# Two products of an attention kernel on smaller tiles of the tensor engine: softmax times v in two column tiles, p' times w_in in eight tiles of 64 rows and 32 columns

## The chip, the cores and the metric

The kernel runs on one core of a Trainium2 chip. The time is device microseconds from start to end. Three runs of the kernel before gave 1541.19 to 1542.47, with a median of 1541.99. All data is fp32. In the profile PE is the tensor engine (PEld its weight loads), DVE the vector engine, ACT the scalar engine, POOL the GpSimd engine, SP the engine that issues most DMAs.

## The reference

Attention through 32 packed queries, then two feed-forward layers. The attention has 8 batches, 8 heads, 576 positions, 64 dimensions a head:

```python
def sm_attn(qq, kk, vv):
    s = scale * np.matmul(qq, kk.transpose(0, 1, 3, 2))
    s = s - np.max(s, axis=-1, keepdims=True)
    a = np.exp(s)
    a = a / (np.sum(a, axis=-1, keepdims=True) + 1e-09)
    return np.matmul(a, vv)
p_packed = sm_attn(p, k, v)            # p' : 32 x 64 for each head
out = sm_attn(q, p_packed, p_packed)   # 576 x 64 for each head
```

The output, as x of 4608 x 512, goes through `h = x @ w_in` (512 x 2048), a rational function of h, `@ w_out`, and then a second layer of the same sizes with a PReLU.

## The kernel before, in words

The second softmax's rows have 32 elements, one for each packed query. The kernel doesn't multiply them by p' and then by w_in; it multiplies p' of each head by that head's 64 rows of w_in once (the products W), and the first MoE layer then multiplies the softmax by this result. So h comes from a matrix of 256 rows (8 heads x 32) for each batch.

The attention runs in units. There are 16 half batches i of four heads, that is two pairs of heads (j = 0, 1 within the unit), and the loop over k (0 to 17) emits in every unit k work of several half batches, in the order of the letters in `ORDER`. For PE, DVE and ACT this comes to:

- s1 of half batch k (L308): scores of the packed queries, four products of 64 columns; DVE takes the maximum (`nm`), ACT the exp.
- T of k-1 (L320): five PE transposes of the exp, copied by ACT and DVE to `a1T`.
- P of k-2 (L333): exp times v. `pp` holds 128 rows (two pairs of heads of 2 x 32 queries) by 256 columns (four heads of 64), of which only the blocks of a head with itself are of use. DVE multiplies by the reciprocal of the sum and by a mask of zeros and ones (`ppn`, two operations of 64 rows). The result has, for a pair of heads, zeros where a head would meet the other's columns.
- R of k-2 (L347): PE transposes `ppn`, DVE copies it to `pph`.
- s2 of k-3 (L357): q times p'; DVE transposes in blocks of 32 (`trn`), takes the maximum, POOL subtracts it.
- E of k-4: ACT's exp, DVE's sums and reciprocal. A and B of k-5: DVE's product and transposes, SP's store to `a2_d`.
- W, four slots in each unit, here called slots 1 to 4: slot 1 stands behind s1, slot 2 behind E, slot 3 behind P, slot 4 behind s2.
- w: one step of the splitting of w_in or w_out (ACT and DVE, some POOL). In units 10 to 14 these are w_out's.
- K, V, Q: SP's loads of k, v and q.

The W products come in groups of 16 for a pair of batches. Units 6 to 9 emit those of the first pair (`emit_Wb0`, L395), units 10 to 13 those of the second, units 14 to 17 those of the third. The fourth pair's (`LAST`) are emitted in the drain (the list `DRAIN`) and in the first two steps of the MoE (`FILL`). From the second pair on, one product (L421) is a 128 x 128 block of p' (two batches, a pair of heads, half of it zeros) by 128 x 512 of w_in into one PSUM bank; ACT (in the last pair ACT and DVE by turns) copies it to `wbs`, and two such halves of 512 columns are stored together. The PSUM pool `psw` has two banks, so a slot's product waits until the bank of two slots before has been copied out.

Every engine works its instructions in the order in which they are emitted; waits are on semaphores. SP, too, issues its DMAs in order, and an issue that waits for data holds back those behind it.

The first MoE's loop starts with `load_a2(0)`, `split_a2(0)` and then L572; from there on nothing of the change is left but the last six W slots.

Of the kernel before, what the change touches and what calls it, by code (L numbers as in the profile page):

```python
# [11 lines left out]
F32 = mybir.dt.float32  # L12
# [4 lines left out]
AF = mybir.ActivationFunctionType  # L17
ALU = mybir.AluOpType
# [10 lines left out]
def attention_then_two_moes(ctx, tc, qT, kT, v, pT, w_in, w_out, ab, w2_in, w2_out, alpha, out):  # L29
    nc = tc.nc  # L30
    mm = nc.tensor.matmul
    act = nc.scalar.activation
    dve = nc.vector
    pool = nc.gpsimd
# [11 lines left out]
    LAST = B // 2 - 1  # L46
# [5 lines left out]
    wp = ctx.enter_context(tc.tile_pool(name="wp", bufs=8))  # L52
# [43 lines left out]
    opened = {}  # L96

    def open_pool(name, **kw):
        opened[name] = ExitStack()
        return opened[name].enter_context(tc.tile_pool(name=name, reuse_waits="tile", **kw))  # L100
# [4 lines left out]
    gp = open_pool("gp", bufs=1, side="left")  # L105
# [93 lines left out]
    spw = open_pool("spw", bufs=2, side="right")  # L199
    psw = open_pool("psw", bufs=2, space=PSUM, side="right")  # L200
    sp0 = open_pool("sp0", bufs=2, side="left")
    ps0 = open_pool("ps0", bufs=1, space=PSUM, side="left")

    ident = sp0.tile([128, 128], F32, tag="ident", name="ident", bufs=1)
    make_identity(nc, ident)
    mask = sp0.tile([128, 128], F32, tag="mask", name="mask", bufs=1)
    pool.memset(mask, 0.0)
    for h in range(4):
        o = 64 * (h % 2)
        pool.memset(mask[32 * h:32 * h + 32, o:o + 64], 1.0)  # L210

    pt, kt, qt, vt = {}, {}, {}, {}

# [21 lines left out]
    w_in_t = {}  # L235

    BLOCKS = [(j, c) for cp in (0, 2) for j in range(4) for c in (cp, cp + 1)]
    EARLY = NF // 2
    w_jobs = [(w_in[128 * j:128 * j + 128, 512 * c:512 * c + 512], plain, w_in_slot, True) for j, c in BLOCKS]
    w_done = []  # L240
# [52 lines left out]
    ps1, a1, rs1, a1T, ppn, ppt, pps, pph, tr, sm, a2 = ({} for _ in range(11))  # L293
# [4 lines left out]
    D = 3  # L298
# [34 lines left out]
    def emit_PP(i):  # L333
        pb = ps0.tile([128, 512], F32, tag="pp", name="pp")
        pps[i] = pb
        pp = pb[:, 0:256]
        at, v_ = a1T.pop(i), vt.pop(i)
        for c in range(5):
            kc = 128 if c < 4 else 64
            mm(pp, at[0:kc, c, :], v_[0:kc, c, :], start=c == 0, stop=c == 4)  # L340
        ppn[i] = sp0.tile([128, 128], F32, tag="ppn", name="ppn", bufs=1)
        for j in range(2):
            r = slice(64 * j, 64 * j + 64)
            dve.scalar_tensor_tensor(ppn[i][r, :], in0=pp[r, 128 * j:128 * j + 128],
                                     scalar=rs1[i][r, :], in1=mask[r, :], op0=ALU.mult, op1=ALU.mult)

    def emit_PPT(i):  # L347
        b, t = divmod(i, 2)
# [39 lines left out]
        b, t = divmod(i, 2)  # L388
        nc.sync.dma_start(out=a2_d[b][:, t, :], in_=a2.pop(i))

    wbs, stores = {}, []

    def emit_Wb0(n):


        f, bi = divmod(n, 2)
        pw = psw.tile([128, 2, 256], F32, tag="wb", name="pw")
        o = 256 * (f % 2)
        for jj, kt in COL:
            mm(pw[64 * jj:64 * jj + 64, kt, :], pph[0][:, 2 * kt + jj, bi, :],  # L400
               w_in_t[2 * kt + jj, f // 2][:, o:o + 256], start=True, stop=True)
        whole_t[bi, f] = wb_slot(NP * bi + f)
        t = whole_t[bi, f].rearrange("p h (k f) -> p h k f", k=2)
        act(t[:, 0], pw, AF.Copy)
        dve.tensor_tensor(t[:, 1], pw, t[:, 0], op=ALU.subtract)
        wb_t[bi, f] = t[:, 0], t[:, 1]

    def emit_Wb(n):
        bp, r = divmod(n, 16)
        if bp == 0:  # L410
            return emit_Wb0(n)
        j, fc = BLOCKS[r]
        if bp == LAST and r % 4 > 1 and "ps0" in opened:
            if fc % 2 == 0:
                wbs[1] = ps0.tile([128, 2, 512], F32, tag="s1", name="pw")
            pw = wbs[1][:, fc % 2, :]
        elif bp == LAST and r % 4 > 1:
            pw = psw2.tile([128, 512], F32, tag="wb", name="pw")
        else:
            pw = psw.tile([128, 512], F32, tag="wb", name="pw")  # L420
        mm(pw, pph[bp][:, j].rearrange("p a b -> p (a b)"), w_in_t[j, fc], start=True, stop=True)  # L421
        if fc % 2 == 0:
            if bp == LAST and r > 0:
                wbs[0] = wp.tile([128, 1024], F32, tag="D", name="wbs")
            elif bp == LAST or len(w_done) == len(w_jobs) and n % 4 == 0:
                wbs[0] = gp.tile([128, 1024], F32, tag="s4", name="wbs", bufs=3)
            else:
                wbs[0] = spw.tile([128, 1024], F32, tag="wbs", name="wbs")
        o = 512 * (fc % 2)
        if bp == LAST and n % 2:  # L430
            dve.tensor_copy(wbs[0][:, o:o + 512], pw)
        else:
            act(wbs[0][:, o:o + 512], pw, AF.Copy)  # L433
        if fc % 2:
            stores.append((bp, j, fc, wbs[0]))

    def store_Wb():
        while stores:
# [8 lines left out]
    def wb_step(k):  # L447
        store_Wb()
        n = nwb[0]
        if n < 16 * LAST and len(w_done) >= (16 if n >= 16 else 8 * (n // 8) + 8) and 4 * (n // 16) + 6 <= k:  # L450
            emit_Wb(n)
            nwb[0] += 1

    def each(f, i):
# [8 lines left out]
    stages = {  # L463
        "V": lambda k: each(load_v, k - 1), "Q": lambda k: each(load_q, k - D + 1), "K": lambda k: each(load_k, k + 2),
        "1": lambda k: each(emit_s1, k), "T": lambda k: each(emit_T, k - 1), "P": lambda k: each(emit_PP, k - 2),
        "R": lambda k: each(emit_PPT, k - 2), "2": lambda k: each(emit_s2, k - D), "E": lambda k: each(emit_exp2, k - D - 1),
        "A": lambda k: each(emit_a2, k - D - 2), "B": lambda k: each(store_a2, k - D - 2), "W": wb_step,
# [15 lines left out]
    for c in range(NCH):  # L483
        o, now = 0, []
        for i, n in enumerate(SHARES[c % 3]):
            b = VISITS[c + i]
# [49 lines left out]
    for c in DRAIN.split():  # L536
        if c == "W":
            store_Wb()
            emit_Wb(nwb[0])
            nwb[0] += 1  # L540
        elif c == "L":
            load_a2(0)
        elif c == "l":
            split_a2(0)
        elif c == "o":
            load_late(len(late_st))
        else:
            {"A": emit_a2, "B": store_a2, "S": emit_s2, "E": emit_exp2, "Q": load_q}[c[0]](NQ - int(c[1]))
# [9 lines left out]
    psw2 = open_pool("psw2", bufs=2, space=PSUM, side="right")  # L558
# [274 lines left out]
    for g in range(NG + LAG):  # L833
# [4 lines left out]
        if g < NG:  # L838
            c, f = divmod(g, NP)
            if f == 1 and c + 1 < NCH:  # L840
                load_a2(c + 1)
            emit_L1(g)
            for _ in range(FILL[g] if g < len(FILL) else 0):
                emit_Wb(nwb[0])
                nwb[0] += 1
# [185 lines left out]
    for u in range(len(units) + 2):  # L1031
        if u < len(units):
            s, y, i, n = units[u]
# [18 lines left out]
            if y == 0:  # L1052
                for g in range(2):
                    q = 0
                    for x, z in PASSES:
                        for k in range(2):
                            mm(ps[:, g, 0:m], w[:, g, x, 128 * k:128 * k + 128], ysp[s, i](z, k),  # L1057
                               start=not onto and q == 0, stop=q == 5, skip_group_check=again)
                            q += 1
            else:  # L1060
                t = vsp.pop(u)
                for g in range(2):
                    for d in range(2):
# [64 lines left out]
```

## Time and profile before

| | |
|---|---|
| median of three runs | 1541.99 us |
| profiled execution | 1541.61 us, span 1539.8 us |
| PE busy | 1472.9 us (96%) |
| DVE busy | 1307.6 us (85%) |
| ACT busy | 1029.5 us (67%) |
| POOL busy | 563.2 us (37%) |
| attention and drain | from 0 to about 206 us |
| first unit with L421 | from 99.34 us (unit 10) |
| first product of the MoE (L572) | at 189.18 us |

The span reaches from the first to the last instruction, and the profiled execution's own time is 1.8 us longer. From 206 us on PE is busy for 1307 of 1334 us. Units 6 to 9 begin with s1 at 61.58, 71.29, 80.64 and 89.99 us, units 10 to 14 at 99.34, 108.62, 119.57, 130.98 and 140.94, unit 15 at 150.60; units 16 and 17 have no s1 and begin at 159.78 and 167.74, the drain at 175.16. An fp32 product shows as two PE records (and two weight loads), a transpose as one.

### The profile page before, as it was taken

Reading aid. Unit: us, or ns where it says so; the run is one execution under the profiler, and the core shown is the slowest. Engines: PE = TensorE matmul, PEld = TensorE weight load, DVE = VectorE, ACT = ScalarE, POOL = GpSimd, SP = SyncE. Lnnn points to the kernel's source line nnn. Section 1 sums busy time; section 2 is a strip of 40 time slices with the busy share of each in tenths; the row PEclk is TensorE's granted clock in tenths of the full one; section 3 lists DMA queues with packets and bytes.
Section 4 is the critical chain, followed back from the end, with each engine's and each line's share of the span. In section 5 each row is a group of like instructions: output and inputs, shape, how many; then the busy total and the mean of one; then the engine's idle time right before and its main releaser. Section 6 shows DMA issues by size and latency. Waiting matters only on the chain.

```text
span 1539.8 us, 20601 instructions
## 1 busy us (share of the span) xinstructions
PE 1472.9 (96%) x7552; PEld 1214.8 (79%) x7552; DVE 1307.6 (85%) x1428; ACT 1029.5 (67%) x1193; POOL 563.2 (37%) x338
## 2 busy tenths in 40 slices
PE   4798879999999999999999999999999999999998
PEld 2454467888888888888888877888888888888898
DVE  5989789898988998999999799968965996599586
ACT  5456488888988888888886676447534743474363
POOL 1223168788788768887664520000000000000000
PEclk9999989999999999999999999999999999999999
DMA  9798964325443533434335877997567656765694
GB/s 348 275 314 265 316 209 130 96 82 178 142 132 121 173 104 117 139 101 137 110 110 183 310 267 234 367 382 292 180 221 286 198 186 217 256 193 200 217 408 172
DMA packets 151108, 322.23 MB, mean 209 GB/s; under 512 B 14816, under 2 KB 79328, under 8 KB 149984
## 3 DMA queue, kind: packets, MB, share of 16 engines
q1 hardware_dynamic: 147552, 308.34, 58.3%
q10 hardware_dynamic: 3456, 12.58, 2.3%
q8 instruction: 60, 0.98, 0.3%
q14 instruction: 40, 0.33, 0.1%
HBM read 230.17 MB, written 90.70 MB: 208 GB/s over the span
## 4 chain that ended last, share of the span: by engine, by line
PE 55%; DVE 15%; ACT 13%; POOL 7%; issue 5%; DMA 4%; SPq 1%; ACTq 0%; POOLq 0%; DVEq 0%
PE p L1065 20%; PE p L1057 20%; PE acc L651 6%; PE h L572 4%; DVE s L91 2%; POOL s L705 2%; DMA qt<-in_qT 1%; DVE s L94 1%; DVE s L88 1%; PE pw L421 1%; PE pp L340 1%; POOL wb L522 1%; ACT h L629 1%; ACT wb L521 1%; DVE v L900 1%
## 5 line engine op out<-in xcount | busy, mean ns | idle before, releaser
L651 PE MATMUL acc<-gt,wo 128*128 128x512 f32 x1728 | 404.9, 390 | 7.0 <-ACT yo L588 7.0
L651 PEld LDWEIGHTS acc<-gt,wo 128*128 128x128 f32 x1728 | 320.1, 188 | 71.2 <-ACT yo L588 8.3
L1057 PE MATMUL p<-ysp,ws 128*128 128x512 f32 (+1 forms) x1680 | 346.9, 368 | 2.9 <-ACT vsp L985 2.4
L1065 PE MATMUL p<-vsp,ws 128*128 128x512 f32 (+1 forms) x1680 | 346.5, 368 | 0.2 <-DVE vsp L986 0.2
L1057 PEld LDWEIGHTS p<-ysp,ws 128*128 128x128 f32 x1680 | 292.5, 189 | 56.8 <-ACT vsp L985 3.4
L1065 PEld LDWEIGHTS p<-vsp,ws 128*128 128x128 f32 x1680 | 292.3, 189 | 53.7 <-DVE vsp L986 1.5
L572 PEld LDWEIGHTS h<-a2t,wb 128*128 128x128 f32 x1728 | 230.0, 194 | 30.3 <-issue 18.5
L572 PE MATMUL h<-a2t,wb 128*128 128x192 f32 (+2 forms) x1728 | 236.3, 293 | 17.3 <-DVE v__1851 L636 5.6
L985 ACT ACTIVATE vsp<-v 128x1024 fp32r<-128x1024 f32 (+1 forms) x140 | 135.7, 971 | 147.6 <-PE p L1065 98.4
L986 DVE TENSOR_TENSOR vsp<-v,vsp 128x1024 fp32r<-128x1024 f32 (+1 forms) x140 | 155.7, 1112 | 32.4 <-ACT vsp L985 31.9
L900 DVE TENSOR_TENSOR v<-v,p 128x1024 f32<-128x1024 f32 (+1 forms) x100 | 110.7, 1109 | 40.7 <-PE p L1057 40.4
L917 DVE SCALAR_TENSOR_TENSOR v<-r,nalpha,v 128x512 f32<-128x512 f32 (+1 forms) x160 | 112.3, 742 | 29.7 <-ACT v L912 29.7
L911 ACT ACTIVATE r<-v 128x1024 f32<-128x1024 f32 (+1 forms) x60 | 58.3, 972 | 76.3 <-DVE v L900 75.9
L900 DVE TENSOR_TENSOR v<-v 128x1024 f32<-128x1024 f32 (+1 forms) x80 | 88.3, 1109 | 0.0
L522 POOL TENSOR_TENSOR wb<-s,wb 128x512 fp32r<-128x512 f32 x48 | 64.7, 1348 | 31.0 <-ACT wb L521 30.5
L88 DVE TENSOR_SCALAR s<-s 128x512 f32<-128x512 f32 x48 | 63.8, 1328 | 0.6 <-ACT s L83 0.6
L912 ACT ACTIVATE v<-v 128x1024 f32<-128x1024 f32 (+1 forms) x60 | 58.6, 976 | 1.9
L91 DVE SCALAR_TENSOR_TENSOR s<-s,s 128x512 int32<-128x512 int32 x40 | 56.8, 1419 | 0.3
L925 ACT ACTIVATE v<-p 128x1024 f32<-128x1024 f32 (+1 forms) x20 | 18.9, 943 | 53.3 <-PE p L1057 53.3
L369 POOL TENSOR_TENSOR trn<-trn,mx 128x576 f32<-128x576 f32 x16 | 20.3, 1268 | 90.9 <-DVE mx L368 80.6
L900 DVE TENSOR_TENSOR c<-c,p 128x1024 f32<-128x1024 f32 (+1 forms) x25 | 27.4, 1112 | 29.9 <-PE p L1065 29.6
L421 PE MATMUL pw<-w_in,pph 128*128 128x512 f32 x96 | 48.5, 619 | 3.9 <-ACT wbs L433 3.9
(1024 smaller groups left out, 2260.6 us busy)
## 6 DMA issues: line engine op xcount, KB each, us to landing
ws<-wh_d SPq DMA_DIRECT2D x224, 512.0 KB, 5.6
wh_d<-ws SPq DMA_DIRECT2D x56, 512.0 KB, 5.0
wq_d<-s SPq DMA_DIRECT2D x32, 512.0 KB, 3.9
wst<-wq_d SPq DMA_DIRECT2D x56, 256.0 KB, 3.9
wb_d<-wbs SPq DMA_DIRECT2D x48, 256.0 KB, 4.5
s<-in_w_out SPq DMA_DIRECT2D x24, 512.0 KB, 4.4
s<-wb_d SPq DMA_DIRECT2D x48, 256.0 KB, 4.2
kt<-in_kT SPq DMA_DIRECT2D x16, 576.0 KB, 7.9
```

The lines of the kernel that those rows point to most:

```text
L88: dve.tensor_scalar(w, w, 0.0, HIGH_R, op0=ALU.max, op1=ALU.min)
L91: dve.scalar_tensor_tensor(wi, in0=wi, scalar=3, in1=low, op0=ALU.logical_shift_left, op1=ALU.bitwise_or)
L421: mm(pw, pph[bp][:, j].rearrange("p a b -> p (a b)"), w_in_t[j, fc], start=True, stop=True)
L522: pool.tensor_tensor(t[:, 1], st, t[:, 0], op=ALU.subtract)
L572: mm(h[:, ft, o:o + m], w[x][:, k, 128 * ft:128 * ft + 128], a2_t[c][:, y, k, o:o + m], start=n == 0, stop=n == 5)
L651: mm(acc[d // 2][:, d % 2, :], w[:, x, 128 * d:128 * d + 128], t[:, y, ft, :], start=f == 0 and (x, y, ft) == (0, 0, 0), stop=f == NP - 1 ...
L900: dve.tensor_tensor(o, a, b, op=op)
L917: dve.scalar_tensor_tensor(v_[:, g], in0=r[:, g], scalar=nalpha[:, f:f + 1], in1=v_[:, g], op0=ALU.mult, op1=ALU.add)
L985: act(t[:, 0, :, 0:m], src, AF.Copy)
L986: return lambda: dve.tensor_tensor(t[:, 1, :, 0:m], src, t[:, 0, :, 0:m], op=ALU.subtract)
L1057: mm(ps[:, g, 0:m], w[:, g, x, 128 * k:128 * k + 128], ysp[s, i](z, k), start=not onto and q == 0, stop=q == 5, skip_group_check=again)
L1065: mm(ps[:, d, 0:m], w[:, g, x, 128 * d:128 * d + 128], t[:, z, g, 0:m], start=not onto and n == 0 and g == 0 and q == 0, stop=n == 3 and g ...
```

## The change

P: the two pairs of heads are multiplied apart, each 64 columns of `a1T` by its own 128 columns of v, into the upper and the lower half of the same 128 columns of PSUM. There are ten products of 128 rows by 64 columns with 128 streamed columns instead of five of 128 by 128 with 256. One DVE operation of 128 rows makes `ppn`; the mask has three blocks of 64 columns, of which a half batch uses two.

W from the second pair of batches on: at an even slot the products of two pairs of heads (x = 0, 1) for one block of 512 columns are emitted together, as eight products of 64 rows (one head) by 32 columns (its packed queries) with 512 streamed columns, four into each of two banks. The odd slot has no product any more; each slot copies one bank out, as before. In half of the pairs of heads the columns of the two heads are turned round (`TURN`), so that the eight tiles lie on different rows and columns of the array; the host lays p out to fit. Two `wbs` tiles fill side by side; they are full behind slots 3 and 4, where the two of before were full behind 2 and 4. `emit_Wb0`, s1, T, R and s2 are as they were.

```diff
-        pp = pb[:, 0:256]
+        pp = pb[:, 0:128]
...
-            mm(pp, at[0:kc, c, :], v_[0:kc, c, :], start=c == 0, stop=c == 4)
+            for j in range(2):
+                mm(pp[64 * j:64 * j + 64, :], at[0:kc, c, 64 * j:64 * j + 64], v_[0:kc, c, 128 * j:128 * j + 128],
+                   start=c == 0, stop=c == 4)
...
-        for j in range(2):
-            r = slice(64 * j, 64 * j + 64)
-            dve.scalar_tensor_tensor(ppn[i][r, :], in0=pp[r, 128 * j:128 * j + 128],
-                                     scalar=rs1[i][r, :], in1=mask[r, :], op0=ALU.mult, op1=ALU.mult)
+        dve.scalar_tensor_tensor(ppn[i], in0=pp, scalar=rs1[i], in1=mask[:, i % 2:i % 2 + 2, :].rearrange("p a b -> p (a b)"), op0=ALU.mult, op1=ALU.mult)
...
+    TURN = (0, 1, 1, 0)
...
-        j, fc = BLOCKS[r]
...
-        mm(pw, pph[bp][:, j].rearrange("p a b -> p (a b)"), w_in_t[j, fc], start=True, stop=True)
+        j0, fc = 2 * (r // 4 % 2), 2 * (r // 8) + r % 4 // 2
+        if r % 2 == 0:
...
+                for x in range(2):
+                    pws[x] = (psw2 if bp == LAST and r % 4 > 1 else psw).tile([128, 512], F32, tag="wb", name="pw")
+            for q in range(4):
+                for x in range(2):
+                    bi, h = q // 2, q % 2
+                    rows, c = slice(64 * h, 64 * h + 64), 32 * (h ^ TURN[j0 + x])
+                    mm(pws[x][64 * bi + c:64 * bi + c + 32, :], pph[bp][rows, j0 + x, bi, c:c + 32],
+                       w_in_t[j0 + x, fc][rows, :], start=True, stop=True)
+        x = r % 2
...
-            act(wbs[0][:, o:o + 512], pw, AF.Copy)
+            act(wbs[x][:, o:o + 512], pws[x], AF.Copy)
         if fc % 2:
-            stores.append((bp, j, fc, wbs[0]))
+            stores.append((bp, j0 + x, fc, wbs[x]))
```

On PE, in unit 14, from behind s1 to R (pw is W, pp<-vt is P, pst and the first ps row T, ps<-qt s2, pp<-ident R; the brackets name the engine or DMA queue that an instruction waits for), the order before is:

```order
L421 MATMUL pw<-w_in,pph 128x512 [waits Activation_49] x2
L340 MATMUL pp<-vt,a1T 128x256 [waits DMAHW2_49,DVE_49]
L340 MATMUL pp<-vt,a1T 128x256 x3
L340 MATMUL pp<-vt,a1T 128x256 [waits DMAHW3_49]
L421 MATMUL pw<-w_in,pph 128x512 [waits Activation_49]
L325 MATMUL pst<-ident,a_1279 128x128 x4
L326 MATMUL ps_1364<-ident,a_1279 64x128
L361 MATMUL ps_1432<-qt,pph 64x288 [waits DMAHW6_49]
L361 MATMUL ps_1432<-qt,pph 64x288 x3
L421 MATMUL pw<-w_in,pph 128x512 [waits Activation_49]
L351 MATMUL pp<-ident,ppn 128x128 [waits DVE_49]
```

And in the changed kernel:

```order
L423 MATMUL pw<-w_in,pph 32x512 [waits Activation_49]
L423 MATMUL pw<-w_in,pph 32x512 [waits PE_49,Activation_49]
L423 MATMUL pw<-w_in,pph 32x512 x6
L340 MATMUL pp<-vt,a1T 64x128 [waits DMAHW2_49,DVE_49]
L340 MATMUL pp<-vt,a1T 64x128 x7
L340 MATMUL pp<-vt,a1T 64x128 [waits DMAHW3_49]
L340 MATMUL pp<-vt,a1T 64x128
L423 MATMUL pw<-w_in,pph 32x512 [waits Activation_49] x2
L423 MATMUL pw<-w_in,pph 32x512 x6
L324 MATMUL pst<-ident,a_1361 128x128 x4
L325 MATMUL ps_1462<-ident,a_1361 64x128
L359 MATMUL ps_1546<-qt,pph 64x288 [waits DMAHW4_49]
```

The W product that stood behind s2, with its wait for ACT, now stands ahead of T, and slot 3 has two waits for ACT (one for each bank) where it had one.

On SP, in unit 15, the DMA issues before are (vt, qt: loads of v and q; wb: stores of W; a_d: the store of B):

```order
L227 DMA vt<-in_v 128x4x256
L228 DMA vt<-in_v 64x256
L441 DMA wb_d_80<-wbs 64x1024
L441 DMA wb_d_81<-wbs 64x1024
L233 DMA qt<-in_qT 128x2x576
L441 DMA wb_d_80<-wbs 64x1024
L441 DMA wb_d_81<-wbs 64x1024
L389 DMA a_d_105<-a_1460 128x576
```

And in the changed kernel:

```order
L226 DMA vt<-in_v 128x4x256
L227 DMA vt<-in_v 64x256
L232 DMA qt<-in_qT 128x2x576
L445 DMA wb_d_80<-wbs 64x1024
L445 DMA wb_d_81<-wbs 64x1024
L445 DMA wb_d_80<-wbs 64x1024
L445 DMA wb_d_81<-wbs 64x1024
L387 DMA a_d_105<-a_1574 128x576
```

The load of q stands ahead of both stores of the unit.

## Rows read from the trace of the kernel before

**Rows 1.** Busy time by stretch: us, engines, PE clock, DMA share, GB/s.

```profile
62.00:100.00 38.00, 38.00 (x262) 22.67 (x259) 34.80 (x79) 16.79 (x32) 6.56 (x6) 1.00 0.94 315
100.00:151.00 51.00, 46.92 (x202) 23.88 (x200) 45.75 (x100) 33.32 (x64) 18.23 (x15) 1.00 0.90 290
151.00:175.00 24.00, 24.00 (x98) 12.35 (x95) 17.93 (x40) 10.09 (x19) 3.47 (x3) 1.00 0.96 308
175.00:206.00 31.00, 22.46 (x91) 12.78 (x90) 21.91 (x33) 18.87 (x25) 7.95 (x5) 0.96 0.93 309
```

**Rows 2.** Timeline of PE, unit 9: start us, us, operation, records.

```profile
89.99 1.19 PE L312 MATMUL ps<-kt,pt 128*64 128x288 f32 x8
91.02 1.90 PE L400 MATMUL pw<-w_in,pph 128*64 128x256 f32 x16
92.84 2.62 PE L340 MATMUL pp<-vt,a1T 128*128 128x256 f32 x10
95.39 1.08 PE L400 MATMUL pw<-w_in,pph 128*64 128x256 f32 x8
```

**Rows 3.** Timeline of PE, records begun from 90.0 to 90.2 us.

```profile
89.99 0.46 PE L312 MATMUL ps<-kt,pt 128*64 128x288 f32 x2
```

**Rows 4.** Timeline of PE, unit 10.

```profile
99.34 1.19 PE L312 MATMUL ps<-kt,pt 128*64 128x288 f32 x8
100.47 1.98 PE L421 MATMUL pw<-w_in,pph 128*128 128x512 f32 x4
102.29 2.52 PE L340 MATMUL pp<-vt,a1T 128*128 128x256 f32 x10
104.73 1.12 PE L421 MATMUL pw<-w_in,pph 128*128 128x512 f32 x2
105.69 0.60 PE L325 MATMUL pst<-ident,a 128*128 128x128 f32 x4
...
106.33 1.19 PE L361 MATMUL ps<-qt,pph 128*64 128x288 f32 x8
107.45 1.13 PE L421 MATMUL pw<-w_in,pph 128*128 128x512 f32 x2
```

**Rows 5.** Groups by line, DVE, 60 to 180 us: busy us, mean ns, idle before.

```profile
L344 DVE SCALAR_TENSOR_TENSOR ppn<-pp,rs,mask 64x128 f32<-64x128 f32 x25 | 8.3, 331 | 0.5 <-PE pp L340 0.3
```

**Rows 6.** Timeline of ACT, units 12 to 14; in brackets idle before and releaser.

```profile
128.10 1.07 ACT L433 ACTIVATE wbs<-pw 128x512 f32<-128x512 f32 x2
...
138.48 1.06 ACT L433 ACTIVATE wbs<-pw 128x512 f32<-128x512 f32 x2
...
148.27 0.63 ACT L282 ACTIVATE wo<-s 128x512 fp32r<-128x512 f32 x1 [1.49 <-DVE sm L376]
148.81 1.06 ACT L433 ACTIVATE wbs<-pw 128x512 f32<-128x512 f32 x2
```

**Rows 7.** Timeline of DVE, units 12 to 15: transposes of s2, maximum of s1.

```profile
130.92 0.82 DVE L365 STREAM_TRANSPOSE trn<-ps 128x288 f32<-128x288 f32 x2
...
140.79 0.82 DVE L365 STREAM_TRANSPOSE trn<-ps 128x288 f32<-128x288 f32 x2
...
149.58 0.82 DVE L365 STREAM_TRANSPOSE trn<-ps 128x288 f32<-128x288 f32 x2
...
151.84 0.76 DVE L315 TENSOR_REDUCE nm<-ps 128x1 f32<-128x576 f32 x1 [0.45 <-PE ps L312]
```

**Rows 8.** Timeline of PE, drain and first MoE; in brackets idle before.

```profile
186.90 2.84 PE L421 MATMUL pw<-w_in,pph 128*128 128x512 f32 x6 [1.92 <-ACT wbs L433]
189.18 3.67 PE L572 MATMUL h<-a2t,wb 128*128 128x192 f32 x24
...
205.72 5.51 PE L572 MATMUL h<-a2t,wb 128*128 128x192 f32 x24 [4.62 <-DVE v__1780 L636]
...
247.60 4.93 PE L572 MATMUL h<-a2t,wb 128*128 128x192 f32 x24 [2.19 <-DVE v__2066 L636]
```

**Rows 9.** Busy time by stretch, 248 to 250 us, columns as in rows 1.

```profile
248.00:250.00 2.00, 2.00 (x10) 2.00 (x9) 1.96 (x3) 1.59 (x3) 1.38 (x1) 0.50 0.24 94
```

More of the change, by code (lines that the diff above doesn't have):

```diff
@@ L205, in attention_then_two_moes @@
     make_identity(nc, ident)
-    mask = sp0.tile([128, 128], F32, tag="mask", name="mask", bufs=1)
+    mask = sp0.tile([128, 3, 64], F32, tag="mask", name="mask", bufs=1)
     pool.memset(mask, 0.0)
-    for h in range(4):
-        o = 64 * (h % 2)
-        pool.memset(mask[32 * h:32 * h + 32, o:o + 64], 1.0)
+    for h, c in ((0, 0), (0, 2), (1, 1), (2, 1), (3, 0), (3, 2)):
+        pool.memset(mask[32 * h:32 * h + 32, c, :], 1.0)
     pt, kt, qt, vt = {}, {}, {}, {}
@@ L389, in store_a2 @@
         nc.sync.dma_start(out=a2_d[b][:, t, :], in_=a2.pop(i))
-    wbs, stores = {}, []
+    TURN = (0, 1, 1, 0)
+    wbs, stores, pws = {}, [], {}
     def emit_Wb0(n):
@@ L411, in emit_Wb @@
             return emit_Wb0(n)
-        j, fc = BLOCKS[r]
[L413 to L420, printed above, removed]
-        mm(pw, pph[bp][:, j].rearrange("p a b -> p (a b)"), w_in_t[j, fc], start=True, stop=True)
+        j0, fc = 2 * (r // 4 % 2), 2 * (r // 8) + r % 4 // 2
@@ new lines, in emit_Wb @@
+        if r % 2 == 0:
+            if bp == LAST and r % 4 > 1 and "ps0" in opened:
+                two = ps0.tile([128, 2, 512], F32, tag="s1", name="pw")
+                pws[0], pws[1] = two[:, 0, :], two[:, 1, :]
+            else:
+                for x in range(2):
[6 more added lines that the diff above has]
+                       w_in_t[j0 + x, fc][rows, :], start=True, stop=True)
@@ L422, in emit_Wb @@
+        x = r % 2
         if fc % 2 == 0:
             if bp == LAST and r > 0:
-                wbs[0] = wp.tile([128, 1024], F32, tag="D", name="wbs")
-            elif bp == LAST or len(w_done) == len(w_jobs) and n % 4 == 0:
-                wbs[0] = gp.tile([128, 1024], F32, tag="s4", name="wbs", bufs=3)
+                wbs[x] = wp.tile([128, 1024], F32, tag="D", name="wbs")
+            elif bp == LAST or len(w_done) == len(w_jobs) and x == 0:
+                wbs[x] = gp.tile([128, 1024], F32, tag="s4", name="wbs", bufs=3)
@@ L427, in emit_Wb @@
             else:
-                wbs[0] = spw.tile([128, 1024], F32, tag="wbs", name="wbs")
+                wbs[x] = spw.tile([128, 1024], F32, tag="wbs", name="wbs")
         o = 512 * (fc % 2)
-        if bp == LAST and n % 2:
-            dve.tensor_copy(wbs[0][:, o:o + 512], pw)
+        if bp == LAST and x:
+            dve.tensor_copy(wbs[x][:, o:o + 512], pws[x])
         else:
-            act(wbs[0][:, o:o + 512], pw, AF.Copy)
+            act(wbs[x][:, o:o + 512], pws[x], AF.Copy)
@@ L1105 @@
     for h2 in range(2):
-        pT[:, h2, :, :, h2, :] = p[:, h2::2].transpose(0, 3, 1, 2)
+        for turn in range(2):
+            j = np.array([turn, 3 - turn])
+            pT[:, h2, :, j, h2 ^ turn, :] = p[:, 2 * j + h2].transpose(1, 0, 3, 2)
     arrays = {
```

## The prediction

> **What bounds the kernel now.** I read the table by stage first, then the tensor engine's (PE's) timeline of single units, then ACT's and DVE's in the same units. The change touches only what runs before 206 us; after that nothing is moved, so what counts is how much earlier or later that point comes. Before it four stretches differ [rows 1]. In 62 to 100 (units 6 to 9) PE is busy 38.00 of 38.00 us: it sets the pace. In 100 to 151 (units 10 to 14) PE has gaps, and DVE works 45.75 of 51: there DVE and ACT, which also split w_out, hand the work to one another. In 151 to 175 (units 15 to 17) PE is full again, 24.00 of 24.00. In 175 to 206 (the drain and the start of the first MoE) nobody is full; the DMA engines are at 0.93.
>
> **Softmax times v (P), five products to ten.** In unit 9 P runs from 92.84 to 95.39, 2.55 us [rows 2]. Each new product streams half the columns into half the array's columns, so if two run side by side the time halves to 1.28; if they don't it stays 2.55. That 64-column products do run side by side is seen in s1: of its eight records two start at once and are through in 0.46 [rows 3], all eight in 1.19 [rows 2], 0.24 for a further pair. I take 1.45, since twenty weight loads stand where ten did. PE's unit of 9.35 us (89.99 to 99.34) [rows 2, 4] becomes 8.25. DVE's share of such a unit is 34.80 / 38 of 9.35, 8.56, less the one ppn operation that goes, 0.33 [rows 5], 8.23. Two in-order engines with equal loads wait for each other a little: 8.5 a unit, 4 x 0.85 = 3.4 us gained. In units 2 to 5, where DVE paces, only ppn counts, some 0.6.
>
> **The w_in products (W), 16 a pair of batches to 64.** Now two W products, 100.47 to 102.29, cost 1.82 us [rows 4]. The eight new ones fill the array once: at best 0.91, half of that. Going from s1 into W at another tile shape costs 0.10 today (1.13 from 99.34 to 100.47 against 1.03 from 89.99 to 91.02) [rows 2, 4]; I take 1.05 for eight. The other end is two at a time, as in rows 3: four times 0.91, 3.6. The rows show only two side by side, but those overlap wholly, and nothing in them speaks for a limit at two, so I stay near the low end.
>
> The Trainium skill, TensorEngine Tiling (Array Packing), "Tiling Modes", says that a change of tiling mode drains TensorE. Rows 2 and 4 agree, at 0.10 us; a unit has seven such changes instead of four, in ten units 3 us if all lay on the path.
>
> **What the pairing moves.** Both slots' products now stand where the first slot's stood, so slot 3's eight need both banks: they wait for the evictions of slots 1 and 2. Before, slot 3 waited for the first alone, and the wait for the second lay at slot 4, behind T and s2. On ACT slot 2's eviction stands behind the second softmax's exp, and in units 11 to 14 often behind a w_out step that itself waits for DVE (in unit 14 the one at 148.27, after 1.49 us of waiting) [rows 6]. So T and s2, and all that DVE does with s2, now hang on it. From the end of that eviction to DVE's transposes: 0.05 + 1.05 (slot 3) + 0.64 (T, 105.69 to 106.33) + 0.05 + 1.12 (s2, 106.33 to 107.45) [rows 4] + 0.1 = 3.0. The eviction is the first of the two in the row of each unit there [rows 6], so it ends 0.53 after the row's start; DVE's transposes are those of [rows 7]:
> - unit 12: 128.63 + 3.0 = 131.63 against 130.92, 0.7 late;
> - unit 13: 139.01 + 3.0 = 142.01 against 140.79, 1.2 late;
> - unit 14: 149.34 + 3.0 = 152.34 against 149.58, 2.8 late, of which 0.45 is the wait for PE that DVE has at 151.84 anyway.
> Units 10 and 11, worked out in the same way, come out even. Each lateness is handed on, since the next max, exp and eviction start from these transposes: 4.2 us lost. The ppn operation saved is swallowed by these waits.
>
> **The clock.** In these units PE has before slot 3 s1, eight W and P (1.13 + 1.05 + 1.45 = 3.6), and from slot 3 on 1.05 + 0.64 + 1.12 and a short transpose, 3.1. A unit lasts 51 / 5 = 10.2 us, now up to 2.8 more, so PE idles 3.5 to 6, nearly all in one stretch before slot 3. Such stretches are in the trace, later on: after 1.92 us idle PE ran at full speed (186.90), after 2.19 at 1.2 GHz (clock 0.50), and after 4.62 the 24 products of L572 took 5.51 instead of the 3.67 at 189.18 [rows 8, 9]. So slot 3, T and s2 would begin at the low level. The price per unit lies between 0 and 5.51 - 3.67 = 1.84; the idle time being near 4, I take 1.8: four units (11 to 14), 7.2 us lost.
>
> **Units 15 to 17 and the drain.** No w_out steps here, so slot 2's eviction comes early. PE loses 1.1 (P) and 4 x 0.91 - 2 x 1.05 = 1.5 (W) a unit, 2.6 of 8; but then the loop s2, transposes, max, exp, eviction, slot 3, T, s2 becomes the longer. Between 0 (the DMA engines are at 0.96 [rows 1]) and 7.8 I take 4.1, a little over the middle. On SP q's load now stands ahead of the unit's first store instead of behind it, so it no longer waits for slot 2's eviction; the same bytes move, and no load waited long here, so nothing for that. In the drain PE finishes its products some 3 us before the first MoE's operands are there and starts L572 cold: between 0 and 1.84, taken 1.0.
>
> **Sum**, against the profiled execution's 1541.6 (the median is 0.4 above): 1541.6 - 0.6 - 3.4 + 4.2 + 7.2 - 4.1 + 1.0 = 1545.9, say 1546.
>
> **Rivals.**
> - *The clock stays up (faster).* If PE's idle time falls into shorter pieces, 7.2 and 1.0 drop out: 1541.6 - 0.6 - 3.4 + 4.2 - 4.1 = 1537.7. It decides where no stretch is longer than the 1.92 before 186.90 [rows 8]. For it: slot 3's first product waits only for slot 1, and the units' shapes shift. Against: four idle microseconds have to lie somewhere. If the wait too were covered, 4.2 more: 1533.5.
> - *The eight don't run together.* Four at a time: slot 3 costs 0.8 more, twice that at the low clock: 4 x 1.6 + 4 x 0.8 = 9.6, 1555. Two at a time: three times that, 29, 1575. The Trainium skill, TensorE: Matmul & The Clock Gate, Part 3, has matmuls start and end strictly in program order; an fp32 product being two records, the second record of one would hold up the next tile, so two at a time. Rows 3 speak against it: both tiles' first records start together. The same part reports 10.6 times for sixteen tiles, which would be the forecast's case.
> - *Nothing moves.* DMA at 0.90 to 0.96 [rows 1] holds the loads, and what PE saves is waited for there: 1542, give or take 2. Against: in units 6 to 9 PE never waited for a load.
>
> **How the numbers follow.** Forecast 0.45, its own range 1542 to 1551; clock stays up 0.28; eight not together 0.12; nothing moves 0.15. A measurement here tells 0.2%, 3.1 us, from no change, so faster is below 1538.9 and slower above 1545.1. Faster: 0.22 of the second case, 0.04 of the last. Slower: 0.35 of the first, 0.12, 0.02. Same: the rest, 0.25. The range 1535 to 1556 leaves out the covered wait and two at a time.
>
> **What would show it.** Right: P at 1.3 to 1.6 us and eight W at 0.95 to 1.2 at full clock; units 6 to 9 at 8.3 to 8.7; in units 11 to 14 PE waiting for ACT's L437 before the second W group, for 3 us or more, clock 0.5 behind it, and DVE's transposes waiting for s2. Wrong: the clock at 1.00 from 100 to 151; W groups above 1.7; or units 11 to 14 no longer than before.

## The result, and the profile after

The changed kernel takes 1553.97 us (median of six runs, 1551.13 to 1554.22) against 1541.74 (six runs, 1541.19 to 1542.47): ratio 1.0074, 95% interval 1.0062 to 1.0086. It is slower, by 12.2 us where 4.3 were forecast. The profiled execution took 1552.44 us (span 1550.5), 10.8 more than that of before.

The same four stretches, with the columns of [rows 1]:

```profile
62.00:100.00 38.00, 35.32 (x320) 21.09 (x320) 36.06 (x82) 17.66 (x35) 7.62 (x7) 1.00 1.01 341
100.00:151.00 51.00, 38.48 (x316) 15.73 (x316) 36.69 (x79) 28.82 (x55) 15.74 (x13) 0.83 0.81 260
151.00:175.00 24.00, 20.31 (x170) 7.89 (x170) 15.37 (x37) 11.52 (x22) 3.89 (x4) 0.86 0.71 228
175.00:206.00 31.00, 22.69 (x203) 10.04 (x204) 19.02 (x35) 10.79 (x18) 6.74 (x4) 0.83 0.90 293
```

From 100 to 151 us PE, DVE and ACT all do less per microsecond than before, and PE's granted clock falls to 0.83: no engine is full, everybody waits. DVE does 36.69 us of work in the 51 where it did 45.75.

The products themselves became as short as forecast. PE's timeline, units 9 and 10 (answers to [rows 2, 4]):

```profile
91.47 1.41 PE L340 MATMUL pp<-vt,a1T 128*64 128x128 f32 x20
...
96.89 1.19 PE L311 MATMUL ps<-kt,pt 128*64 128x288 f32 x8
98.02 1.25 PE L423 MATMUL pw<-w_in,pph 64*32 64x512 f32 x16
```

From its first record to the end of its last P takes 1.41 us instead of 2.62 [rows 2]. The eight W products take 1.25 us here and 1.09 in most units where both banks are free; two of before took 1.98 [rows 4]. In unit 13 (134.00 below) the records that begin before 134.06 are

```profile
134.00 0.66 PE L423 MATMUL pw<-w_in,pph 64*32 64x512 f32 x8
```

so the first records of all eight products start within 0.06 us. The Trainium skill, TensorE: Matmul & The Clock Gate, Part 3, has matmuls start and end strictly in program order, from which the prediction's second rival took two at a time and 3.6 us. What the trace contradicts is that step: the second record of a product doesn't hold up the next tile.

Unit 13 shows the loss. PE from s1 to R (in brackets idle time before and what ended it):

```profile
132.88 1.19 PE L311 MATMUL ps<-kt,pt 128*64 128x288 f32 x8
134.00 1.09 PE L423 MATMUL pw<-w_in,pph 64*32 64x512 f32 x16
135.02 1.46 PE L340 MATMUL pp<-vt,a1T 128*64 128x128 f32 x20
136.65 1.04 PE L423 MATMUL pw<-w_in,pph 64*32 64x512 f32 x2 [0.17 <-ACT wbs L437]
140.91 1.96 PE L423 MATMUL pw<-w_in,pph 64*32 64x512 f32 x14 [3.22 <-ACT wbs L437]
142.80 1.11 PE L324 MATMUL pst<-ident,a 128*128 128x128 f32 x4
...
144.06 2.13 PE L359 MATMUL ps<-qt,pph 128*64 128x288 f32 x8
```

ACT in the same unit, from the second softmax's exp to slot 2's eviction (the last row):

```profile
136.49 0.68 ACT L370 ACTIVATE trn<-trn 128x576 f32<-128x576 f32 x1
138.65 0.63 ACT L281 ACTIVATE wo<-s 128x512 fp32r<-128x512 f32 x1 [1.48 <-DVE s L94]
139.18 0.65 ACT L83 ACTIVATE s<-raw 128x512 f32<-128x512 f32 x1
139.74 0.66 ACT L84 ACTIVATE raw<-raw 128x512 int32<-128x512 uint8 x1
140.29 0.57 ACT L437 ACTIVATE wbs<-pw 128x512 f32<-128x512 f32 x1
```

And DVE, which needs T's and s2's results:

```profile
144.16 0.28 DVE L329 COPY a1T<-ps 64x128 f32<-64x128 f32 x1 [2.33 <-PE ps L325]
...
146.24 0.85 DVE L363 STREAM_TRANSPOSE trn<-ps 128x288 f32<-128x288 f32 x2 [1.72 <-PE ps L359]
```

Slot 3's first product (two records) needs slot 1's bank and runs at 136.65; its second needs slot 2's, whose eviction stands on ACT behind the exp and a w_out step that itself waits for DVE. It is let go at 140.91. By then PE has been idle for 3.22 us, slot 3, T and s2 run at the low level (2.13 us for s2, 1.19 at full clock), and DVE waits 2.33 and 1.72 us. Before, PE had T and s2 behind it in that time; its s1 of unit 13 began at 130.98:

```profile
137.33 0.60 PE L325 MATMUL pst<-ident,a 128*128 128x128 f32 x4
...
137.97 1.19 PE L361 MATMUL ps<-qt,pph 128*64 128x288 f32 x8
139.10 1.13 PE L421 MATMUL pw<-w_in,pph 128*128 128x512 f32 x2
```

So s2 began 7.0 us after s1 before and begins 11.2 us after it now.

By stages, from the starts of s1 in each unit and of the MoE's first product:

| stretch | before | after | difference | forecast |
|---|---|---|---|---|
| up to unit 6 | 61.58 | 62.19 | +0.6 | -0.6 |
| units 6 to 9 | 37.76 | 34.70 | -3.1 | -3.4 |
| unit 10 | 9.28 | 8.78 | -0.5 | 0 |
| units 11 to 14 | 41.98 | 54.52 | +12.5 | +11.4 |
| units 15 to 17 and drain | 38.58 | 39.20 | +0.6 | -4.1 |
| first product to third (205.72, 216.33) | 16.54 | 16.94 | +0.4 | +1.0 |

### The profile page after: what moved, and what is told of

Its sections match the earlier page's. It is cut to its first block, busy times and chain, and to the rows that moved or that the text cites. A ratio compares the mean times of both kernels' runs of the same rounds, so it can differ in the third digit from the quotient of the medians.

```text
span 1550.5 us, 21490 instructions
## 1 busy us (share of the span) xinstructions
PE 1457.6 (94%) x8000; PEld 1197.6 (77%) x8000; DVE 1300.3 (84%) x1412; ACT 1029.9 (66%) x1193; POOL 563.5 (36%) x340
## 3 DMA queue, kind: packets, MB, share of 16 engines
q8 instruction: 64, 1.05, 0.3%
## 4 chain that ended last, share of the span: by engine, by line
PE 55%; DVE 16%; ACT 12%; POOL 6%; issue 5%; DMA 5%; SPq 0%; ACTq 0%; POOLq 0%; DVEq 0%
PE p L1069 20%; PE p L1061 20%; PE acc L655 7%; PE h L576 4%; DVE s L91 2%; DMA vt<-in_v 2%; POOL s L709 2%; DVE s L94 1%; PE pw L423 1%; DMA qt<-in_qT 1%; DVE s L88 1%; POOL wb L526 1%; DVE v L904 1%; DVE h L639 1%; ACT wb L525 1%
## 5 line engine op out<-in xcount | busy, mean ns | idle before, releaser
L423 PE MATMUL pw<-w_in,pph 64*32 64x512 f32 x384 | 40.2, 712 | 18.0 <-ACT wbs L437 14.5
```

## The experiments

Twelve kernels. The table has the starts (us) on which the readings rest and the granted clock from 100 to 151; "units 11 to 14" is the first two columns' difference, "to the MoE" that of the second and third. Starts come from one execution each, ratios (with 95% intervals) from 4 to 12 runs against runs of before on the same chip. That one execution lies 3.8, 2.5 and 3.6 us below its kernel's median for "slots 2 and 4", "slot 2 early" and "last pair old" and 3.0 above it for "W alone", so a difference of a few us between the stretches of two kernels is firm only where the ratios show it too.

| kernel | s1 of 11 | s1 of 15 | MoE | units 11 to 14 | to the MoE | clock | median | ratio |
|---|---|---|---|---|---|---|---|---|
| before | 108.62 | 150.60 | 189.18 | 41.98 | 38.58 | 1.00 | 1541.74 | 1 |
| after | 105.67 | 160.19 | 199.39 | 54.52 | 39.20 | 0.83 | 1553.97 | 1.0074 [1.0062, 1.0086] |
| P alone | 105.18 | 146.39 | 182.73 | 41.21 | 36.34 | 1.00 | 1537.07 | 0.9964 [0.9952, 0.9977] |
| W alone | 108.57 | 160.70 | 200.07 | 52.13 | 39.37 | 0.90 | 1552.20 | 1.0051 [1.0036, 1.0067] |
| pairs alone | 108.13 | 158.37 | 199.13 | 50.24 | 40.76 | 0.97 | 1551.31 | 1.0053 [1.0040, 1.0066] |
| slots 2 and 4 | 103.94 | 148.03 | 186.02 | 44.09 | 37.99 | 0.87 | 1542.59 | 0.9994 [0.9984, 1.0004] |
| slot 2 early | 105.96 | 147.18 | 184.63 | 41.22 | 37.45 | 0.97 | 1540.56 | 0.9984 [0.9975, 0.9993] |
| slot 3 late | 103.59 | 146.60 | 188.58 | 43.01 | 41.98 | 0.90 | 1542.00 | 0.9999 [0.9989, 1.0008] |
| filler | 105.29 | 151.95 | 189.34 | 46.66 | 37.39 | 1.00 | 1544.63 | 1.0011 [1.0003, 1.0020] |
| slots 2 and 4, filler | 104.44 | 147.83 | 186.24 | 43.39 | 38.41 | 1.00 | 1541.52 | 1.0000 [0.9990, 1.0010] |
| slot 2 early, last pair old | 106.03 | 147.25 | 185.07 | 41.22 | 37.82 | 0.93 | 1542.19 | 0.9996 [0.9988, 1.0005] |
| P, slot 2 early | 106.80 | 148.15 | 185.75 | 41.35 | 37.60 | 0.97 | 1538.84 | 0.9982 [0.9973, 0.9991] |
| slot 2 early, loads first | 104.44 | 147.24 | 182.12 | 42.80 | 34.88 | 0.97 | 1535.46 | 0.9962 [0.9950, 0.9974] |
| P, loads first | 104.36 | 145.59 | 180.18 | 41.23 | 34.59 | 1.00 | 1534.05 | 0.9947 [0.9935, 0.9960] |

The theory: slot 3's wait for slot 2's eviction holds T and s2, and the idle time it makes drops the clock for them. The rivals: P's tiles make PE idle; the small tiles are slow in use; the clock alone, or the wait alone.

**Which part: P alone.** The new P with the old mask; W as before.

```diff
...
-            mm(pp, at[0:kc, c, :], v_[0:kc, c, :], start=c == 0, stop=c == 4)
+            for j in range(2):
+                mm(pp[64 * j:64 * j + 64, :], at[0:kc, c, 64 * j:64 * j + 64], v_[0:kc, c, 128 * j:128 * j + 128],
+                   start=c == 0, stop=c == 4)
...
```

> The kernel before with P alone changed: ten products of 64 columns with one ppn operation; the W products stay 128 x 128, one a slot. Theory (the loss comes from slot 3's wait for slot 2's eviction and from the low clock behind it, both of them W's): units 6 to 9 fall to 8.2 to 8.5 us as in the changed kernel, units 10 to 14 stay within 0.5 us of before's, granted clock 0.97 or more in 100 to 151; 1538 to 1540 us, ratio to before about 0.998. Rival (P's tiles are at fault, since the shorter P makes PE idle long enough for the clock to fall): units 11 to 14 are longer by 4 us or more in all with the clock at 0.9 or lower, 1544 or slower. Rival (the loads of v hold what P saves): 1541 to 1542.

Measured: faster than before, and by a little more than expected: 1537.07 us, 0.9964. Units 11 to 14 take 0.8 us less than before, unit 10 1.0 less (expected was within 0.5 of before), and the clock stays at 1.00; P alone isn't at fault.

**W alone.** The diff of the change without its P part.

> The changed kernel with P put back to five products of 256 streamed columns and two ppn operations; W stays in eight tiles, two pairs of heads at a time. Theory (wait and clock, both W's): slot 3's second product still waits for ACT in units 11 to 14 for some 3 us a unit, clock 0.85 or lower in 100 to 151, 1554 to 1558 us, ratio to before 1.008 to 1.011 (the 3 us that P won in units 6 to 9 are gone, and P's extra 1.1 us a unit may shorten the idle time a little). Rival (the loss needs P's tiles too, which take PE's last cover away): clock 0.95 or higher in 100 to 151, and 1543 to 1547.

Measured: slower, but less than expected (1.0051, not 1.008 to 1.011), and the clock is 0.90, not 0.85 or lower. W carries 10.15 of the 12.54 us of units 11 to 14. P's tiles add 2.4 there although P alone costs nothing. With the shorter P, PE is idle for 14.3 us ahead of slot 3's products in these four units, without it for 9.4 (0.17 and 3.22 of the 14.3 are those of unit 13 above).

**Pairs alone.** P and W in the products of before; at the even slots two of W's 128 x 128 products together.

```diff
...
+        if r % 2 == 0:
...
+                for x in range(2):
+                    pws[x] = (psw2 if bp == LAST and r % 4 > 1 else psw).tile([128, 512], F32, tag="wb", name="pw")
+            for x in range(2):
+                mm(pws[x], pph[bp][:, j].rearrange("p a b -> p (a b)"), w_in_t[j, fc + x], start=True, stop=True)
+        pw = pws[r % 2]
...
```

> The kernel before, P and the 128 x 128 W products as they were, but two W products are emitted together at the even slots (slots 1 and 3), and the odd slots only copy out. Theory (the pairing, which puts slot 3's wait for slot 2's eviction ahead of T and s2, is enough): units 11 to 14 longer by 4 to 10 us in all, with slot 3's second product waiting for ACT for 2 us or more; 1546 to 1552, ratio 1.003 to 1.007; the clock may stay up, since PE has 2.5 us a unit more to do than in the changed kernel. Rival (the tiles are at fault, not the pairing): within 0.2% of before, 1539 to 1545.

Measured: as the theory has it, 1551.31 us. PE, unit 12:

```profile
125.64 0.59 PE L421 MATMUL pw<-w_in,pph 128*128 128x512 f32 x1
128.86 2.07 PE L421 MATMUL pw<-w_in,pph 128*128 128x512 f32 x2 [2.63 <-ACT wbs L434]
130.73 1.06 PE L325 MATMUL pst<-ident,a 128*128 128x128 f32 x4
```

The same wait with the old products, and in units 12 and 14 the low clock behind it: 8.3 us in units 11 to 14. So the order makes most of the loss (8.3 of W's 10.15), and not the tiles. That the tiles need this order is seen in unit 13 above: slot 3's first product, alone, takes 1.04 us, as long as all eight together.

**Taking the wait away, three ways.** First, products and both evictions together at slots 2 and 4:

```diff
         if r % 2 == 0:
+            return
...
+        for x in range(2):
...
```

> The changed kernel with the same tiles, but both banks' evictions are emitted directly behind the eight products, at slots 2 and 4; slots 1 and 3 are empty. So slot 4's products need evictions that were emitted before the unit's P, T and s2, and nothing of T and s2 stands behind that wait. Theory (the place of the wait makes the loss): units 11 to 14 no longer than before's (51 us for 100 to 151 or less), granted clock 0.95 or more, 1535 to 1539 us. Rival (PE's idle time alone drops the clock, wherever the wait stands): clock 0.9 or lower, 1542 to 1548. Rival (the tiles themselves are slow in use): 1552 or slower.

Measured: 10.4 of the 12.5 us are gone. But the clock is 0.87, not 0.95, and the time is on before's, not 1535 to 1539: clock and time are those that the first rival named (0.9 or lower, 1542 to 1548), so this run leaves open what the low clock still costs here. PE in unit 13:

```profile
130.92 1.19 PE L359 MATMUL ps<-qt,pph 128*64 128x288 f32 x8
134.56 2.44 PE L425 MATMUL pw<-w_in,pph 64*32 64x512 f32 x16 [2.45 <-ACT wbs L439]
136.93 0.48 PE L349 MATMUL pp<-ident,ppn 128*128 128x128 f32 x1
```

The wait is still there, and so is the low clock, but s2 (130.92) now stands ahead of both, at 1.19 us.

Second, slot 2 ahead of the exp, so that its eviction is early:

```diff
-    ORDER = "1AKWBwwVEWwPWQwT2WRw"
+    ORDER = "1AKWWBwwVEwPWQwT2WRw"
```

> The changed kernel with slot 2 emitted directly behind slot 1, ahead of the second softmax's exp (E) and of both w_out steps, so that on ACT the eviction which slot 3 waits for no longer stands behind the exp; all products and their order on PE stay. Theory (slot 3's wait for slot 2's eviction makes most of the loss: the paired 128 x 128 products alone cost 8.2 us at a ratio of 1.0053): that wait falls from some 3 us a unit to under 1 in units 11 to 14, these units lose 3 us or less against before instead of 12.5, and the run takes 1538 to 1545 us, ratio to before 0.997 to 1.001. Rival (the idle time of PE as such, through the clock, makes the loss wherever the wait stands): clock in 100 to 151 still 0.85 or lower and 1548 or slower. Rival (an eviction ahead of the exp only hands the lateness to DVE's sums): 1548 or slower with the clock at 0.9 or more.

Measured: 41.22 us for units 11 to 14, 0.8 less than before, clock 0.97; 1540.56 us. One letter moved takes 13 us off the changed kernel.

Third, slot 3 behind s2:

```diff
-    ORDER = "1AKWBwwVEWwPWQwT2WRw"
+    ORDER = "1AKWBwwVEWwPQwT2WWRw"
```

> The changed kernel with slot 3 moved from behind P to behind s2, next to slot 4, so that T and s2 stand ahead of slot 3's wait; tiles, pairs and slots 1, 2 and 4 stay. Theory (the loss comes from T and s2 being held behind that wait): units 11 to 14 within 3 us of before's 42.0, 1537 to 1543 us, ratio to before 0.996 to 1.001, and PE's idle time then lies ahead of slot 3 with nothing but R behind it. Rival (two products at once need both banks, wherever they stand: the eviction of the next unit's slot 1 comes late instead): 1548 or slower. Rival (idle time and clock): 1546 or slower with the clock at 0.85 or lower in 100 to 151.

Measured: 43.01 us in these units, as the theory has it. It is lost again from unit 15 on (41.98 to the MoE). SP waits longer there for evictions of W before it may store them, from 146 to 190 us

```profile
SPq L445 <- ACT wbs L437: 13.5, 5, 5.6
```

where before such waits came to 9.6. Late loads behind these stores don't explain the loss by themselves: from 150 to 190 us PE waits 3.3 us for v and q here, and 4.5 with slot 2 early, whose stretch is 37.45. What the rest is stays open.

**Wait and clock apart.** The wait stays; eight more products (results unused) fill PE's idle time in units 11 to 14:

```diff
+        if 9 <= i <= 12:
+            fill = ps0.tile([128, 2, 512], F32, tag="s2", name="fill")
+            for c in range(FILLER):
+                mm(fill[:, c % 2, 0:256], at[:, c % 4, :], v_[:, c % 4, :], start=True, stop=True)
...
+    FILLER = 8
```

> The changed kernel with eight more fp32 products of 128 x 256 (about 4 us, results unused) on PE behind P in units 11 to 14, where PE otherwise waits for slot 2's eviction; this adds work only. Theory of the forecast (the low clock behind the idle time costs 1.8 us a unit, 7.2 in all): clock in 100 to 151 above 0.95, slot 3's products, T and s2 in 3 us instead of 5.2, and 1545 to 1549 us. Rival (after the pairing alone, the paired 128 x 128 products, lost 8.3 us in units 11 to 14 with the clock at 0.97: the wait costs more than forecast and the clock less, some 2 to 4 us): 1549 to 1553 with the clock above 0.95. Rival (the filler itself is late and delays slot 3): 1554 or slower.

Measured: 3.7 us more work a unit make the kernel 9.3 us faster than the changed one (1544.63). PE, unit 14:

```profile
143.91 3.72 PE L345 MATMUL fill<-vt,a1T 128*128 128x256 f32 x16
147.56 1.04 PE L428 MATMUL pw<-w_in,pph 64*32 64x512 f32 x2
148.85 1.09 PE L428 MATMUL pw<-w_in,pph 64*32 64x512 f32 x14 [0.25 <-ACT wbs L442]
149.87 0.66 PE L324 MATMUL pst<-ident,a 128*128 128x128 f32 x4
...
150.57 1.19 PE L363 MATMUL ps<-qt,pph 128*64 128x288 f32 x8
```

Slot 3 takes 1.09 instead of 1.96, T 0.66 instead of 1.11. Units 11 to 14 fall from 54.52 to 46.66: 7.9 us were the clock's. The rows give the same in another way. From the start of slot 3's second product to the end of s2 it takes 2.91 us here (148.85 to 151.76); in the changed kernel it takes 4.26, 5.11, 5.28 and 5.10 in units 11 to 14, 8.1 more in all. The 4.7 left are the wait's, as far as the filler itself isn't late: slot 3's group begins right behind the filler and takes 0.45 to 1.47 us longer than the 1.09 of eight together in each of the four units, so the eviction sets it and not the filler.

The same filler where the wait holds nothing:

> The kernel with the same tiles whose eight products and both evictions stand together at slots 2 and 4 (0.9994 of before), and in addition eight more fp32 products of 128 x 256 (results unused) behind P in units 11 to 14, as in the run with the filler. Its clock in 100 to 151 was 0.87 and its slot 4 groups took 2.44 us where a group at full clock takes 1.05 to 1.26. Theory (that low clock is what is left of the loss, 1 to 1.3 us a unit): clock above 0.95 and 1537 to 1540 us, 3 to 5 below the same kernel without the filler. Rival (DVE and ACT set these units, so the clock of PE costs nothing there): within 1 us of the kernel without the filler, or slower since the filler takes PE's time.

Measured: the time that the rival named. The clock rises from 0.87 to 1.00 and the units gain 0.7 us of 44.1, the run nothing that can be told. The run settles less than it was meant to, though: in units 13 and 14 PE is now busy for 20.25 of 20.25 us, so the filler itself sets them and may hide what the clock gives back. An upper bound, an estimate, comes from slot 2 early: the same tiles take 41.22 us there, so in the kernel with slots 2 and 4 wait and low clock together cost 2.9. The low clock costs 7.9 us where T and s2 run at it, and at most 2.9 where W, R and the next s1 do.

**The drain and units 15 to 17.** First the last pair's products unpaired, in the kernel with slot 2 early:

```diff
+        if bp == LAST:
...
+            mm(pws[x], pph[bp][:, j0 + x].rearrange("p a b -> p (a b)"), w_in_t[j0 + x, fc], start=True, stop=True)
...
```

> The kernel with slot 2 ahead of E (0.9984 of before), and in it the last pair's W products, those of the drain and of the MoE's first steps, in the old form: one 128 x 128 product a slot, ACT and DVE copying out by turns. It asks what the pairing costs in the drain: with it, the second group of the drain waited 3.62 us for a DVE eviction and ran at the low clock (4.17 us for four groups' records); the stretch from unit 15's s1 to the MoE's first product was 37.45 us there, 36.34 with the old products (the run with P alone), 38.58 in the kernel before. Theory (the pairing waits in the drain as in the units, for an eviction that stands behind the second softmax): that stretch falls to 36 to 36.6 and the run to 1537.5 to 1540. Rival (the drain is set by the loads of q and v and by DVE's second softmax, not by the products): the stretch stays within 0.4 of 37.45, and 1540 to 1542.

Measured: the rival; 37.82 to the MoE instead of 37.45. The pairing isn't what the drain hangs on.

Then the place of slot 2 in the kernel with P alone (the ORDER of slot 2 early):

> P alone changed (0.9964 of before, the products of W 128 x 128 and one a slot), and slot 2 moved ahead of E as in the run that did this to the changed kernel. It asks whether that place is better by itself or only takes away the wait of the paired products. Theory (it only takes away the wait, which single products don't have): within 0.15% of P alone, 1535 to 1540. Rival (an earlier eviction frees DVE and ACT in any form): 1533 to 1535. Rival (slot 2's product and eviction ahead of the exp make the second softmax late where nothing was gained): 1540 or slower.

Measured: no gain. It is 0.18% behind P alone (0.9982 against 0.9964, expected was 0.15% or less; the intervals just touch), units 11 to 14 at 41.35 and 41.21. So the early place brings nothing by itself; it takes away a wait that single products don't have.

Then SP's order, in the kernel with slot 2 early and in that with P alone. The lines are those of the first, against the changed kernel, so they hold slot 2's early place too; in the second V and Q move in the same way and W stays:

```diff
-    ORDER = "1AKWWBwwVEwPWQwT2WRw"
+    ORDER = "1AKVQWWBwwEwPWwT2WRw"
```

> The kernel with slot 2 ahead of E (0.9984 of before), and SP's loads of v and q moved to the head of each unit, behind k's load, so that they no longer stand behind B's store, which waits for DVE, nor behind the stores of W. It asks why what PE saves in units 15 to 17 and the drain didn't come through: P waited there for v's load for 1.84 and 2.62 us, and from unit 15's s1 to the MoE's first product it took 37.45 us. Theory (SP's order makes these loads late): the waits for v and q go, that stretch falls to 34 to 36, and the run to 1535.5 to 1539. Rival (the transfers themselves are at their limit, the DMA engines being at 0.94 in 151 to 175: the bytes come no sooner, and the stores of W or the loads of k are late instead): the stretch stays within 0.7 of 37.45, 1539.5 to 1543. Rival (DVE's second softmax sets these units): the waits for v go, but the stretch stays, and DVE is at 0.75 or more of 151 to 175.

Measured: as the theory has it. PE's waits between 150 and 190 us (total, times, longest) with slot 2 early:

```profile
PE pp L340 <- DMA vt<-in_v: 4.5, 2, 2.6
PE pw L423 <- DVE wbs L435: 3.6, 1, 3.6
```

and with the loads first:

```profile
PE pw L423 <- DVE wbs L435: 3.6, 1, 3.6
PE pp L340 <- DVE pph L353: 1.3, 2, 0.7
```

The wait for v is gone and the stretch is 34.88 us instead of 37.45, at a DMA share of 0.94 from 151 to 175 us in both: the bytes could come earlier, they were issued late.

> P alone changed (0.9964 of before), and SP's loads of v and q moved to the head of each unit, behind k's load. Here only q was waited for (0.56 and 1.30 us in units 17 and the drain), and the stretch from unit 15's s1 to the MoE's first product took 36.34 us. Theory (SP's order makes the loads late): 35 to 36 us for that stretch, 1535 to 1537.5. Rival (the transfers are at their limit): no change, 1536 to 1539. Rival (v and q ahead of the stores and of k's later use take the bandwidth from k in the first units, where the DMA engines are at 0.85 or more): unit 6 begins later than 62.06 by 0.5 us or more, 1538 or slower.

Measured: 1534.05 us, better than expected; 34.59 to the MoE. This is the best of the versions tried: P's column tiles, W's products as in the kernel before, and v and q issued at the head of each unit; 0.9947 of before. Unit 6 begins at 62.20, so the early loads didn't hold up the first units.

## Why the prediction was right in direction and too small

- **P and W side by side: right.** 1.41 to 1.46 us for P (1.45 taken), 1.02 to 1.09 for the eight in most units (1.05). Units 6 to 9 gain 3.1 (3.4), less in unit 7, where P waits 0.90 us for the load of v. In unit 10 it waits 1.78. Groups whose second product waits for its bank take longer at full clock too, 1.93 to 2.14 (units 11, 15 and 16).
- **The wait ahead of T and s2: right in place and size.** 4.2 was forecast for it and the filler leaves 4.7; three kernels that take it from ahead of T and s2 by different means lose 2.1, -0.8 and 1.0 in units 11 to 14 instead of 12.5.
- **The clock: right, with two steps of its working off.** 7.2 against 7.9, forecast from PE's idle time and [rows 8]. Per unit 11 to 14 the sum of both was 1.8, 2.5, 3.0 and 4.2, and the trace has 2.0, 2.9, 3.5 and 4.2 (starts of s1: 105.67, 118.60, 132.88, 146.38, 160.19). The bound of 1.84 a unit, read from L572's 24 products, was too low: slot 3's rest, T and s2 lose 2.2, 2.4 and 2.2 in units 12 to 14, and 1.35 in unit 11, so the sum comes near by luck in part. And slot 3's first product waits too, for slot 1's eviction, so the idle time stands in two pieces. In unit 11 neither is longer than the 1.92 by which the first rival decided, and s2 ran at the low level all the same (2.19):

```profile
111.20 1.04 PE L423 MATMUL pw<-w_in,pph 64*32 64x512 f32 x2 [1.04 <-ACT wbs L437]
114.00 1.09 PE L423 MATMUL pw<-w_in,pph 64*32 64x512 f32 x14 [1.75 <-ACT wbs L437]
...
116.07 2.19 PE L359 MATMUL ps<-qt,pph 128*64 128x288 f32 x8
```

- **Units 2 to 5: sign wrong, small.** +0.6 instead of -0.6. Of the kernels here the eleven with the new P begin unit 6 at 61.50 to 62.55, the three with the old one at 60.85 to 61.58. One ppn operation less doesn't show there. What the traces show is a lower granted clock from 36 to 62 us with the new P (0.79 in the changed kernel, 0.80 with P alone) than with the old (0.87 before, 0.91 with W alone); whether that is the cause wasn't tried.

**Units 15 to 17 and the drain: the step that failed.** The prediction took 4.1 us of gain there, between 0 and 7.8, and for SP: "no load waited long here, so nothing for that". The gain was -0.6, outside its bounds. Units 15 to 17 take 21.71 us instead of 24.56 (the drain begins at 181.90, before at 175.16), 2.9 gained, and the drain loses 3.5. PE there:

```profile
178.10 1.46 PE L340 MATMUL pp<-vt,a1T 128*64 128x128 f32 x20 [1.83 <-DMA vt<-in_v]
...
185.99 1.28 PE L359 MATMUL ps<-qt,pph 128*64 128x288 f32 x8 [3.00 <-DMA qt<-in_qT]
187.20 4.02 PE L423 MATMUL pw<-w_in,pph 64*32 64x512 f32 x32
194.71 4.75 PE L423 MATMUL pw<-w_in,pph 64*32 64x512 f32 x32 [3.48 <-DVE wbs L435]
```

and what SP waited for between 150 and 190 us:

```profile
SPq L387 <- DVE a L383: 12.0, 5, 4.6
SPq L445 <- ACT wbs L437: 8.5, 6, 4.4
```

The loads of v and q stand on SP behind B's store, and that waits for DVE. Before, these waits were

```profile
SPq L389 <- DVE a L385: 5.0, 5, 1.5
SPq L441 <- ACT wbs L433: 6.7, 5, 2.3
```

and PE waited for a load only once:

```profile
PE ps L361 <- DMA qt<-in_qT: 1.3, 1, 1.3
```

When PE gets shorter the loads become the next thing that is late, and they are late by their place in a queue, as the runs with the loads first show. This term is 4.7 of the 6.5 us missing in the sum. From the changed kernel's 39.20 us to the MoE slot 2's early place takes off 1.75, and the loads first another 2.57; the 34.88 left is near the 34.5 that the forecast came to. So what the prediction had wrong there is above all the loads, put at nothing, and beside them, as far as slot 2's early place shows it, the pair's wait. These are differences of single executions, and the loads first in the changed kernel itself weren't tried. That PE hardly waited for a load in the old trace says that it was early enough for the old PE; it bounds nothing for a shorter one. What the 3.48 in the drain is worth by itself stays open: the run with the last pair unpaired didn't get shorter, and with the loads first a wait of 3.6 is still there.

## What to carry to other kernels

The tiles that shared the array here were issued together (one product alone took 1.04 us, eight 1.09), and a pair then needs both its buffers at once: look at what releases the second one, and at what stands behind it in the in-order queue, before counting the array time saved. The idle stretch on PE cost twice here, 4.7 us as the wait and 7.9 as the clock of what ran behind it, so put work that gates another engine ahead of the wait, not behind it. When an engine gets shorter, count for each load when it is issued and not whether it was waited for before.

## What the runs showed that was not expected

- Work added for nothing, 3.7 us a unit on PE, took 9.3 us off the changed kernel's run, since it kept the granted clock from 100 to 151 us at 1.00 instead of 0.83.
- The low clock is cheap or dear by place: 0.87 against 1.00 was worth 2.9 us at most with the wait behind s2 (an estimate, see above), 0.83 against 1.00 7.9 us with the wait ahead of T and s2.
- P's tiles are worth 0.36% alone and nothing with the paired W (1.0074 with them, 1.0051 without, the intervals overlap): gains of two edits didn't add up, and PE's idle time ahead of slot 3 grew from 9.4 to 14.3 us in units 11 to 14.
